# A carried state in 64 columns on four quarters of the array, and weight pieces that begin six rooms after their fetch

## The chip, the core and the metric

The kernel runs on one core of a Trainium2 chip. The core has a matrix engine (TensorE, PE in the profile; its weight loads are PEld), three engines for elementwise work (VectorE is DVE, ScalarE is ACT, GpSimd is POOL) and a queue processor (SyncE, SP) that issues most transfers between the memory of the chip and the on-chip buffer. TensorE writes its results to eight banks of an accumulator memory (PSUM), from which VectorE and ScalarE read them. Every engine works through its own list of instructions in order and waits at semaphores for the others. The metric is the device time of one execution in microseconds (us).

## What is computed

A retention layer with eight heads of 64 features, over two batches of 768 tokens, then two feed-forward layers on the 1536 x 512 result. Cut to what matters:

```python
# retention: per head, causal products with powers of lam, and a state carried from block to block
intra = einsum('bhij,bhjd->bhid', einsum('bhic,bhjc->bhij', qb, kb) * Dmask, vb)
inter = einsum('bhid,bhde->bhie', qb * lam_pow, kv_state)
out[:, :, sl] = intra + inter
kv_state = lam_block * kv_state + einsum('bhsd,bhse->bhde', kb * rev_pow, vb)
...
x = attn_out as [1536, 512]
h = maximum(x @ w_in, 0);  x = (h * h) @ w_out          # 512 -> 2048 -> 512
h = x @ w_in2;  out = maximum(0.01 * h, h) @ w_out2     # 512 -> 2048 -> 512
```

The four weight matrices are 64-bit floating-point numbers in memory.

## The kernel before

**Retention.** The work is cut into 12 units, six chunks of 128 tokens for each of two batches. The eight heads stand in four pairs (`NP` = 4): the two heads of a pair fill the 128 partitions, 64 features (`D`) each. All products here are in fp32, and the trace records each such matmul twice. Per unit there are `transposes` of k and q (line 294, copied to kT and qT by ScalarE on line 298), `scores` (line 311, one bank for each of the two heads of the pairs), `mask` (VectorE, line 316, makes Pm), `state` (line 335: the update of the carried state) and `output`. The state lies in two tiles `st` that alternate from chunk to chunk. They are 128 x 4 x 128: each pair has a 128 x 128 block of which only the two diagonal 64 x 64 blocks are filled and the rest stays zero (memset on line 321). So in `output` the product of the state with the scaled query qS (line 360) takes all 128 rows of the array and 64 of its columns, as the product of v with Pm does (line 362) that is added to it in the same bank; a pair of heads has two of each, one for either half of the columns. The bank is then cast to xhi by ScalarE (line 68) and the rest xlo is taken by VectorE (line 69), `split`. In the loop over the units, `state(i)`, `output(i)`, `mask(i + 1)` and `scores(i + 2)` follow each other on TensorE.

**The two MLPs.** All operands are split in a high and a low part, and each product takes three matmuls of 128 x 128 x 512 (`three`, line 503: high by high, high by low, low by high). Each layer goes through four stages of 512 hidden features; products of a stage go to `activate` (lines 468 to 486), which makes the operands g0h, g0l, g1h, g1l, sw of the second product. Some products are combined by sums and differences of tokens and weights (`four_sums`, lines 449 to 451, `weight_sums`, lines 437 to 442, and `activate_for_seven`, lines 482 to 491), so that fewer are needed.

**Weight pieces.** `fetch` starts the transfer of one 1 MB piece into one of two `raw` buffers. The generator `converting` then turns the 64-bit words to fp32: an absolute value on ScalarE (Abs, line 114), six steps on VectorE (lines 115 to 125), a cast to the high part on ScalarE (line 135) and a subtraction for the low part on VectorE (line 137). `convert` is called once for each room, a place in TensorE's program between half groups of matmuls: it takes the next step of a piece under way, or begins the next one that is fetched. Within the MLPs a piece's step fetches the next piece.

**What sets the order.** In the retention the order on SP and TensorE is the order in which the code is written, and in the MLPs that on TensorE. The order on VectorE, ScalarE and GpSimd is chosen by the framework's scheduler, unless an instruction is held in its place (`keep_in_program_order`), as the conversion steps are that the retention places.

## Time and profile before

| | |
|---|---|
| median of three runs | 576.34 us (575.51 to 576.9) |
| profiled execution | 577.1 us |
| its span, first to last instruction | 575.3 us |
| mean granted TensorE clock, share of full speed | 0.994 |
| TensorE matmul busy | 566.2 us |
| VectorE, ScalarE, GpSimd busy | 413.8, 303.7, 103.3 us |
| first matmul of the MLPs (line 503) starts at | 63.59 us |

All times in the trace are microseconds from the first instruction of the span. A time of the whole execution is 1.8 us more than the span. In a row of a timeline the columns are the start, the time, the engine, the line, the operation, what is written and read, the array shape on TensorE (128\*64 is 128 rows by 64 columns), sizes and the count; in brackets stands how long the engine was idle just before and what ended it. In a row of the chain they are the start, the time and what the time is put down to. The names are those of the program: `ps` a bank, `raw` a fetched piece, `hb` and `rb` a piece under conversion.

### The profile page before, as it was taken

What the parts mean: (1) busy time and instruction counts of PE and PEld (TensorE: products, weight loads), DVE (VectorE), ACT (ScalarE), POOL (GpSimd) and SP (SyncE); (2) the same over time, 40 slices, a digit from 0 to 9 for tenths busy, and PEclk for the clock granted to TensorE, in tenths of its full rate; (3) what the DMA queues carried; (4) which work ended last, traced back from release to release, by engine and by line L of the source; (5) the groups of instructions that cost most, each with busy time, mean ns of one, the idle gap of its engine ahead of it and who ended that gap; (6) DMA issues with size and microseconds to landing.
All of it is one profiled execution on the core that took longest, in us unless ns stands there. A gap on an engine that the chain in (4) does not pass through costs nothing.

```text
span 575.3 us, 8060 instructions
## 1 busy us (share of the span) xinstructions
PE 566.2 (98%) x3075; PEld 472.8 (82%) x3075; DVE 413.8 (72%) x579; ACT 303.7 (53%) x477; POOL 103.3 (18%) x115
## 2 busy tenths in 40 slices
PE   7999999999999999999999999999999999999997
PEld 6888888888788888888888888888888888888886
DVE  3588999999927599498478999929782996217222
ACT  2344598556757587757448375453562376225110
POOL 3659100000044503433000000000213010210000
PEclk9899999999999999999999999999999999999999
DMA  8998434665498957999513215341529423651432
GB/s 173 235 218 177 142 130 140 221 190 186 171 157 137 161 168 176 214 254 188 174 38 91 81 34 216 129 164 73 110 49 246 108 32 43 78 87 56 164 111 91
DMA packets 79350, 80.75 MB, mean 140 GB/s; under 512 B 40264, under 2 KB 51792, under 8 KB 79312
## 3 DMA queue, kind: packets, MB, share of 16 engines
q1 hardware_dynamic: 61312, 62.15, 35.2%
q0 software_dynamic: 17472, 17.83, 22.9%
q8 instruction: 24, 0.39, 0.3%
q10 hardware_dynamic: 528, 0.26, 0.2%
q14 instruction: 14, 0.11, 0.1%
HBM read 55.05 MB, written 30.42 MB: 149 GB/s over the span
## 4 chain that ended last, share of the span: by engine, by line
PE 79%; DVE 10%; DMA 5%; issue 3%; ACT 2%; POOL 1%; SPq 0%; ACTq 0%; POOLq 0%; DVEq 0%
PE ps L503 72%; DMA raw<-in_moe_w_in 4%; PE ps L294 2%; DMA raw<-in_moe_w_out 2%; DVE hb L118 2%; PE ps L311 1%; DVE rb L122 1%; DVE hb L125 1%; PE ps L362 1%; DVE hb L115 1%; DVE rb L121 1%; PE ps L335 1%; ACT hb L114 1%; PE ps L220 1%; PE ps L360 1%
## 5 line engine op out<-in xcount | busy, mean ns | idle before, releaser
L503 PE MATMUL ps<-xhi,w1h 128*128 128x512 f32 x288 | 112.2, 389 | 0.0
L503 PE MATMUL ps<-xhi,w1l 128*128 128x512 f32 x288 | 112.0, 389 | 0.0
L503 PE MATMUL ps<-xlo,w1h 128*128 128x512 f32 x288 | 112.0, 389 | 0.0
L616 POOL DMA_DIRECT2D spill<-f x48 | 47.1, 1194 | 348.3 <-ACT f L612 348.2
L612 ACT COPY f<-ps 128x512 f32<-128x512 f32 x84 | 48.4, 585 | 69.6 <-PE ps L503 68.8
L503 PEld LDWEIGHTS ps<-xhi,w1l 128*128 128x128 f32 x288 | 54.1, 188 | 11.3
L503 PEld LDWEIGHTS ps<-xlo,w1h 128*128 128x128 f32 x288 | 54.1, 188 | 11.3
L503 PEld LDWEIGHTS ps<-xhi,w1h 128*128 128x128 f32 x288 | 54.0, 188 | 11.3 <-issue 0.2
L474 DVE TENSOR_TENSOR g0l<-f,g0h 128x512 fp32r<-128x512 f32 x52 | 35.1, 687 | 32.5 <-ACT f L470 20.9
L503 PE MATMUL ps<-w2l,g0h 128*128 128x512 f32 (+1 forms) x132 | 50.5, 383 | 0.0
L503 PE MATMUL ps<-w2h,g0l 128*128 128x512 f32 (+1 forms) x132 | 50.5, 383 | 0.0
L503 PE MATMUL ps<-w2h,g0h 128*128 128x512 f32 (+1 forms) x132 | 50.5, 383 | 0.0
L114 ACT ACTIVATE hb<-raw 128x1024 f32<-128x1024 f32 x32 | 36.8, 1149 | 21.5 <-DVE w2l L137 8.3
L137 DVE TENSOR_TENSOR w2l<-hb,w2h 128x1024 fp32r<-128x1024 f32 x16 | 19.5, 1222 | 39.8 <-ACT w2h L135 39.8
L503 PE MATMUL ps<-g0h,w2h 128*128 128x512 f32 x104 | 40.5, 389 | 0.0
L503 PE MATMUL ps<-g0l,w2h 128*128 128x512 f32 x104 | 40.5, 389 | 0.0
L503 PE MATMUL ps<-g0h,w2l 128*128 128x512 f32 x104 | 40.5, 389 | 0.0
L122 DVE SCALAR_TENSOR_TENSOR rb<-raw,rb 128x1024 f32<-128x1024 uint32 x32 | 39.4, 1231 | 0.4
L125 DVE TENSOR_TENSOR hb<-hb,rb 128x1024 f32<-128x1024 f32 x32 | 39.4, 1231 | 0.4
L118 DVE SCALAR_TENSOR_TENSOR hb<-raw,hb 128x1024 uint32<-128x1024 uint32 x32 | 39.1, 1221 | 0.3
L567 DVE TENSOR_TENSOR f<-ps,f 128x512 f32<-128x512 f32 x40 | 26.2, 684 | 9.9 <-PE ps L503 9.9
L716 DVE TENSOR_TENSOR f<-ps,f 128x512 f32<-128x512 f32 (+1 forms) x25 | 16.7, 668 | 22.9 <-PE ps L503 22.8
(143 smaller groups left out, 1155.0 us busy)
## 6 DMA issues: line engine op xcount, KB each, us to landing
raw<-in_moe_w_in SPq DMA_DIRECT2D x16, 1024.0 KB, 5.7
raw<-in_moe_w_out SPq DMA_DIRECT2D x16, 1024.0 KB, 5.1
spill<-f POOLq DMA_DIRECT2D x48, 256.0 KB, 5.5
spill<-f SPq DMA_DIRECT2D x24, 256.0 KB, 2.8
f<-spill SPq DMA_DIRECT2D x24, 256.0 KB, 3.0
k<-in_k SPq DMA_DIRECT2D x12, 256.0 KB, 5.0
q<-in_q SPq DMA_DIRECT2D x12, 256.0 KB, 5.1
v<-in_v SPq DMA_DIRECT2D x12, 256.0 KB, 5.3
```

Of the source, the lines that this page charges most:

```text
L114: nc.scalar.activation(hf, w_hi.bitcast(F32), AF.Abs)
L118: yield ve.scalar_tensor_tensor(out=hb, in0=w_hi, scalar=0xC0000000, in1=hb, op0=ALU.bitwise_and, op1=ALU.bitwise_or)
L122: yield ve.scalar_tensor_tensor(out=rf, in0=w_lo, scalar=2.0 ** -52, in1=rf, op0=ALU.mult, op1=ALU.mult)
L125: yield ve.tensor_tensor(out=hf, in0=hf, in1=rf, op=ALU.add)
L137: yield ve.tensor_tensor(out=lo, in0=hf, in1=hi, op=ALU.subtract)
L294: nc.tensor.transpose(ps[:, p, :], src[:, 2 * p:2 * p + 2, :].rearrange("s h d -> s (h d)"), ident)
L474: nc.vector.tensor_tensor(out=glo, in0=r, in1=ghi, op=ALU.subtract)
L503: nc.tensor.matmul(ps, a, b, start=start and n == 0, stop=stop and n == len(ops) - 1, skip_group_check=again)
L567: ve.tensor_tensor(out=out, in0=ps[h, where], in1=other, op=ALU.add)
L612: nc.scalar.copy(f, src)
L616: nc.gpsimd.dma_start(dst, f, accum_op=ALU.add)
L716: nc.vector.tensor_tensor(out=a, in0=ps, in1=a, op=ALU.add)
```

## The change

The state tiles become 128 x 4 x 64: the blocks of the two heads of a pair lie in the upper and the lower 64 partitions, and there is no memset. The state is updated with one GpSimd and one VectorE operation on 128 partitions, where there were two each on 64.

In `output` the eight state products come first, then the eight value products. A state product now uses one quarter of the array, 64 rows by 64 columns: the rows are those of the head in its pair, the columns are the same half for even pairs and the other half for odd pairs. The output lies in two banks, even pairs in one and odd pairs in the other, and is split in two halves. For odd pairs the two halves of the 128 features are therefore swapped in xhi and xlo. To match, a piece of the first layer's w_in is fetched with three transfers: the even 128 rows in place, and for the odd ones each half of 64 rows to the other half of the partitions.

A fetched piece carries the count of rooms at which it may begin: six (`LAND`) after its fetch in the MLPs, and at once in the retention. The Abs is held in program order.

```diff
+    half = [slice(e * D, (e + 1) * D) for e in range(2)]
...
-            dma(r.rearrange("p (k f) -> p k f", k=k), source(*key))
-            fetched.append((key, r))
+            dst, src = r.rearrange("p (k f) -> p k f", k=k), source(*key)
+            if key[0] or key[2]:
+                dma(dst, src)
+            else:
+                dma(dst[:, 0:k:2], src[:, 0:k:2])
+                for a, b in ((half[0], half[1]), (half[1], half[0])):
+                    dma(dst[a, 1:k:2], src[b, 1:k:2])
+            fetched.append((key, r, len(rooms) + LAND if begun_mlp else 0))
...
-        nc.scalar.activation(hf, w_hi.bitcast(F32), AF.Abs)
+        tc.keep_in_program_order(nc.scalar.activation(hf, w_hi.bitcast(F32), AF.Abs))
...
     def convert(pin=False):
+        rooms.append(len(rooms))
...
-        if not fetched:
+        if not fetched or len(rooms) < fetched[0][2]:
             return
...
-            st.append(att.tile([P, NP, P], F32, name=f"st{e}"))
-            nc.gpsimd.memset(st[e], 0.0)
+            st.append(att.tile([P, NP, D], F32, name=f"st{e}"))
...
-                for par in range(2):
-                    r = slice(par * D, (par + 1) * D)
-                    nc.gpsimd.tensor_tensor(out=tmp[r], in0=old[r, :, r],
-                                            in1=LR[r, :, C - 1:C].to_broadcast([D, NP, D]), op=ALU.mult)
...
+                nc.gpsimd.tensor_tensor(out=tmp, in0=old, in1=LR[:, :, C - 1:C].to_broadcast([P, NP, D]), op=ALU.mult)
+                nc.vector.tensor_tensor(out=new, in0=ps, in1=tmp, op=ALU.add)
...
-            ps = bank().rearrange("p (a s) -> p a s", a=NP)
-            for p in range(NP):
-
-                rows = [slice(par * D, (par + 1) * D) for par in range(2)]
-                if c:
-                    for r in rows:
-                        nc.tensor.matmul(ps[r, p, :], st[c % 2][:, p, r], qS[n][:, p, :], start=True, stop=False)
-                for par, r in enumerate(rows):
-                    nc.tensor.matmul(ps[r, p, :], vn[:, 2 * p + par, :], Pm[n][:, par, p, :], start=c == 0, stop=True)
+            ps = [bank()[:, 0:2 * C].rearrange("p (a s) -> p a s", a=2) for _ in range(2)]
+            heads = [(p, par ^ p % 2) for p in range(NP) for par in range(2)]
+
+            def place(p, par):
+                return ps[p % 2][half[par ^ p % 2], p // 2, :]
+
+            if c:
+                for p, par in heads:
+                    nc.tensor.matmul(place(p, par), st[c % 2][half[par], p, :], qS[n][half[par], p, :],
+                                     start=p < 2, stop=False, skip_group_check=True)
+            for p, par in heads:
+                nc.tensor.matmul(place(p, par), vn[:, 2 * p + par, :], Pm[n][:, par, p, :],
+                                 start=c == 0, stop=True, skip_group_check=True)
...
-            split(xhi[t][:, :, o:o + C], xlo[t][:, :, o:o + C], ps)
+            for e in range(2):
+                split(xhi[t][:, e::2, o:o + C], xlo[t][:, e::2, o:o + C], ps[e])
```

Where this moves instructions is shown at three places, each as it stands before and then after. On TensorE, one unit of the retention: the scores, the transposes of a later unit, the state update and the output, of which before only the first of four pairs of heads stands here. (In these rows a name is what is written, then what is read, then the size of the result and how many in a row.)

```order
L311 MATMUL ps<-qT,kT 128x128 x8
L294 MATMUL ps<-ident,k 128x128 x4
L294 MATMUL ps<-ident,q 128x128 x4
L335 MATMUL ps<-v,kd 64x64 x8
L360 MATMUL ps<-qS,st_168 64x128 x2
L362 MATMUL ps<-Pm,v 64x128 x2
```

```order
L322 MATMUL ps<-qT,kT 128x128 x8
L305 MATMUL ps<-ident,k 128x128 x4
L305 MATMUL ps<-ident,q 128x128 x4
L345 MATMUL ps<-v,kd 64x64 x8
L366 MATMUL ps<-qS,st_168 64x128 x8
L369 MATMUL ps<-Pm,v 64x128 x8
```

The pairs of state and value products have become eight of one and then eight of the other. On ScalarE in the retention, where the first weight piece begins:

```order
L68 CAST xhi_278<-ps 128x4x128
L114 ACTIVATE hb<-raw 128x1024
L298 COPY kT<-ps 128x512
L298 COPY qT<-ps 128x512
L68 CAST xhi_278<-ps 128x4x128
```

```order
L68 CAST xhi_276<-ps 128x2x128 x2
L309 COPY kT<-ps 128x512
L309 COPY qT<-ps 128x512
L68 CAST xhi_276<-ps 128x2x128 x2
L124 ACTIVATE hb<-raw 128x1024
L309 COPY kT<-ps 128x512
L309 COPY qT<-ps 128x512
```

The Abs (L114, now L124) has moved behind the copies of kT and qT and the next unit's casts. On VectorE near the end of the second stage of the first MLP layer, the last of the sums by `activate_for_seven` (L491, now L500) and the subtraction that makes g1l (L69) from its cast:

```order
L488 TENSOR_TENSOR g0l<-f,g0h 128x512
L125 TENSOR_TENSOR hb<-hb,rb 128x1024
L491 TENSOR_TENSOR f<-f 128x512
L437 TENSOR_TENSOR rb<-hb 128x256
L438 TENSOR_TENSOR rb<-hb 128x256
L439 TENSOR_TENSOR rb<-rb,hb 128x256
L440 TENSOR_TENSOR rb<-hb,rb 128x256
L69 TENSOR_TENSOR g1l<-f,g1h 128x512
```

```order
L497 TENSOR_TENSOR g0l<-f,g0h 128x512
L131 TENSOR_SCALAR rb<-hb 128x1024
L500 TENSOR_TENSOR f<-f 128x512
L132 SCALAR_TENSOR_TENSOR rb<-raw,rb 128x1024
L69 TENSOR_TENSOR g1l<-f,g1h 128x512
L135 TENSOR_TENSOR hb<-hb,rb 128x1024
```

The four sums of a weight piece (L437 to L440) have left the place between them, and one conversion step (L132) stands there. The order of the matmuls in the MLPs is the same in both kernels.

## Rows read from the trace of the kernel before

**Rows 1.** The page: busy time, share of the span and instructions by engine

```profile
PE 566.2 (98%) x3075; PEld 472.8 (82%) x3075; DVE 413.8 (72%) x579; ACT 303.7 (53%) x477; POOL 103.3 (18%) x115
```

**Rows 2.** Waits of TensorE: us in total, times, longest

```profile
PE ps L335 <- POOL qS L304: 2.4, 1, 2.4
...
PE ps L503 <- DVE g1l L69: 0.9, 1, 0.9
```

**Rows 3.** The chain that ended last, from 64 us: its last piece

```profile
155.74 415.73 PE ps L503 x1844
```

**Rows 4.** Busy us of PE, PEld, DVE, ACT, POOL in two stretches of the MLPs

```profile
62.60:100.00 37.40, 37.40 (x179) 30.95 (x176) 36.91 (x48) 30.67 (x46) 0.00 (x0) 1.00 0.35 114
...
130.00:160.00 30.00, 29.08 (x128) 23.51 (x127) 29.45 (x42) 20.72 (x37) 1.03 (x1) 1.00 0.52 171
```

**Rows 5.** The chain from 14 to 64 us: units of the retention

```profile
33.86 1.03 PE ps L294 x8
34.88 0.61 PE ps L335 x16
35.50 0.22 PE ps L360 x4
35.72 0.22 PE ps L362 x4
...
37.25 1.09 PE ps L311 x16
...
39.36 0.37 PE ps L360 x4
...
43.99 0.88 PE ps L362 x16
```

**Rows 6.** TensorE's timeline, starts of outputs and of the scores behind them

```profile
26.12 0.39 PE L360 MATMUL ps<-qS,st 128*64 128x128 f32 x4
...
27.97 1.16 PE L311 MATMUL ps<-qT,kT 64*128 64x128 f32 x16
...
30.60 0.39 PE L360 MATMUL ps<-qS,st 128*64 128x128 f32 x4
...
32.69 1.16 PE L311 MATMUL ps<-qT,kT 64*128 64x128 f32 x16 [0.17 <-ACT qT L298]
```

**Rows 7.** ScalarE's timeline at the first weight piece

```profile
30.52 1.16 ACT L114 ACTIVATE hb<-raw 128x1024 f32<-128x1024 f32 x1 [1.85 <-DMA raw<-in_moe_w_in]
```

**Rows 8.** SP's timeline: issues of transfers

```profile
22.73 1.29 SPq L65 DMA_DIRECT2D raw<-in_moe_w_in  x1
...
26.00 4.25 SPq L65 DMA_DIRECT2D v<-in_v  x1
```

**Rows 9.** The tile v from 20 to 40 us: from issue to landing

```profile
DMA to landing us min/median/max: 4.8/5.8/7.3
```

**Rows 10.** TensorE's timeline from 153 to 157 us

```profile
153.95 0.88 PE L503 MATMUL ps<-g1h,sw 128*128 128x512 f32 x2
155.74 0.50 PE L503 MATMUL ps<-g1l,sw 128*128 128x512 f32 x1 [0.92 <-DVE g1l L69]
156.08 0.63 PE L503 MATMUL ps<-g1h,sw 128*128 128x512 f32 x2
```

**Rows 11.** VectorE's timeline in the same place

```profile
152.93 0.69 DVE L491 TENSOR_TENSOR f<-f 128x512 f32<-128x512 f32 x1
153.53 0.42 DVE L437 TENSOR_TENSOR rb<-hb 128x256 f32<-128x256 f32 x1
...
155.00 0.69 DVE L69 TENSOR_TENSOR g1l<-f,g1h 128x512 fp32r<-128x512 f32 x1
```

**Rows 12.** ScalarE's timeline in the same place

```profile
153.65 0.62 ACT L68 CAST g1h<-f 128x512 fp32r<-128x512 f32 x1 [1.82 <-DVE f L491]
```

**Rows 13.** VectorE from 64 to 170 us, groups: busy, mean ns

```profile
L122 DVE SCALAR_TENSOR_TENSOR rb<-raw,rb 128x1024 f32<-128x1024 uint32 x11 | 13.4, 1219 | 0.1
...
L115 DVE TENSOR_SCALAR hb<-hb 128x1024 f32<-128x1024 f32 x10 | 6.9, 687 | 0.4 <-ACT hb L114 0.4
```

**Rows 14.** ScalarE from 64 to 170 us, groups: busy, mean ns

```profile
L135 ACT CAST w2h<-hb 128x1024 fp32r<-128x1024 f32 x5 | 5.3, 1051 | 1.7 <-PE ps L503 0.9 <-DVE hb L125 0.7
```

More of the change, by code (lines that the diff above doesn't have):

```diff
@@ L86, in tile_retention_then_two_mlps @@
     todo = list(order)
-    fetched, at_work = [], []
+    fetched, at_work, rooms = [], [], []
+    LAND = 6
     wts, sums, opened = {}, {}, set()
@@ L94, in fetch @@
             k = 4 if key[2] == 0 else 2
-            dma(r.rearrange("p (k f) -> p k f", k=k), source(*key))
-            fetched.append((key, r))
+            dst, src = r.rearrange("p (k f) -> p k f", k=k), source(*key)
[6 more added lines that the diff above has]
+            fetched.append((key, r, len(rooms) + LAND if begun_mlp else 0))
     def converting():
-        key, r = fetched.pop(0)
+        key, r, _ = fetched.pop(0)
         l, s, n, h = key
@@ L339, in state @@
                 tmp = wk.tile([P, NP, D], F32, tag="tmp", name="tmp")
-                for par in range(2):
-                    r = slice(par * D, (par + 1) * D)
-                    nc.gpsimd.tensor_tensor(out=tmp[r], in0=old[r, :, r],
-                                            in1=LR[r, :, C - 1:C].to_broadcast([D, NP, D]), op=ALU.mult)
-            for par in range(2):
-                r = slice(par * D, (par + 1) * D)
-                if c:
-                    nc.vector.tensor_tensor(out=new[r, :, r], in0=ps[r], in1=tmp[r], op=ALU.add)
-                else:
-                    nc.vector.tensor_copy(new[r, :, r], ps[r])
+                nc.gpsimd.tensor_tensor(out=tmp, in0=old, in1=LR[:, :, C - 1:C].to_broadcast([P, NP, D]), op=ALU.mult)
+                nc.vector.tensor_tensor(out=new, in0=ps, in1=tmp, op=ALU.add)
+            else:
+                nc.vector.tensor_copy(new, ps)
         def output(n):
```

1 line of the change is left out of this document (removed).

## The prediction

> **What bounds the kernel now.** I read the busy shares of the page first: TensorE works 98% of the span [rows 1]. Then the table of its waits: two places stand out, 2.4 us in the first units, where the mask is not there yet, and 0.9 us in the long stage [rows 2]. The first lies ahead of all state products, and the change touches nothing that it waits for, so it stays. Third, the chain that ended last: from 155.74 on it is one piece of 1844 matmuls in 415.73 us, 0.2255 us each, with no hole [rows 3]. The number and order of these matmuls do not change. So a gain or loss can come from three places only: from the time TensorE spends per matmul in the retention (the chain from 14 to 64 us), from its few waits, and from waits that the new order of the other engines brings in. For the last, I looked at engine times by stage: VectorE is busy 36.91 of 37.40 us and 29.45 of 30 us in the two stretches of the first MLP stages that I show [rows 4], so it has no room there, though TensorE itself lacks only 0.92 us in the second.
>
> **Part 1, the state product.** In the chain each fp32 matmul is two records. One output of before takes four pairs of lines L360 and L362, each line 0.22 us for four records [rows 5], so its eight state products cost 4 x 0.22 = 0.88 us and its eight value products as much; alone they also take 0.88, at 43.99 [rows 5]. With an array half (128 rows by 64 columns) two of these run at once. On quarters four can, so eight take half: 0.44 us. The eight state updates of line L335, with half the columns, take 0.61 [rows 5], of which I put 0.15 down to the switch of shape before them (below); the rest, 0.46, shows that 16 records can be issued in that time. So the state products come to 0.44 to 0.46, a gain of 0.42 to 0.44.
>
> Against it stand switches of shape. A first L360 line after the transposes takes 0.37 where later ones take 0.22 [rows 5]: 0.15 for a change of shape. After L335, whose shape is the same as that of L360, the first line takes 0.22: no price. In after, the state products have a shape of their own, so an output that follows a state update pays twice (into quarters, and back to halves), one that follows transposes pays once more than now. Ten outputs have a state: two after transposes (units 1 and 5), seven after a state update, the last after the value products of the one before it. Eight gain 0.43 - 0.30 = 0.13, two gain 0.43 - 0.15 = 0.28: together **1.6 us**. What the trace does not show is a switch into quarters. Bounds: free, as from L335 to L360, all ten would gain 0.44, together 4.4; at 0.22, the dearest that I find (1.09 for the scores [rows 5], against 0.87 for eight matmuls two at a time), 2 x 0.22 = 0.4. I take 0.15, since transposes to halves is the nearest row.
>
> The state's smaller tile spares memsets, a GpSimd and a VectorE operation for each unit; an output is cast and split in two halves, one operation more on ScalarE and on VectorE. TensorE waits in the retention for none of these [rows 2], so I cost them at nothing; if that cover goes, a unit pays about one half operation.
>
> **Part 2, the absolute value held in place.** At 30.52 ScalarE starts the first piece's Abs, 1.16 us, after it has stood idle for a transfer [rows 7]; copies of the transposed k and q queue behind it, and the scores at 32.69 wait 0.17 for qT [rows 6]. From the start of an output to that of the next scores it is 1.85 us without a wait (26.12 to 27.97), and 2.09 here (30.60 to 32.69) [rows 6]: **0.24 us** lost. In after the Abs stands behind the next unit's casts. It finds its data there, and the copies that queue behind it then are wanted by scores 1.85 us of output later, so the wait goes: 0.24. For that piece SP issues three transfers where one was, with loads of k, q, v queued behind them. The one issue takes 1.29; the load of v that follows is itself held at 26.00 for 4.25 us, while the transfers ahead of it run [rows 8], and lands 7.3 us after its issue at the latest, at 33.3 [rows 9], while its first user runs at 34.88 [rows 5]. With TensorE some 0.8 us earlier there, 0.8 of that cover is left. Two more issues cost nothing while they vanish in the 4.25; wholly exposed (2 x 1.29) they would cost 2.6 - 0.8 = 1.8 us, my bound.
>
> **Part 3, pieces begun six rooms later.** The 0.9 of the waits table is more than 0.9. Around it, five matmuls (two, one and two) take from 153.95 to 156.08 + 2 x 0.227 = 156.53: 2.58 us instead of 5 x 0.227 = 1.13, a loss of **1.45 us** [rows 10]. The operand g1l that the middle one awaits is a subtraction on VectorE. Its input was cast on ScalarE from 153.65 to 154.27 [rows 12], but VectorE ran four sums of a weight piece from 153.53 to 155.00 first [rows 11], which is needed much later. In after's order those sums are elsewhere, and between the operation that feeds the cast and the subtraction stands one L132, the L122 of before, 1.22 us [rows 13], which covers the cast of 0.62. So this wait goes, 1.45 us. What is late next? The second half of the first w_out piece: its cast follows matmul 119 of the stage's count and its first use is matmul 150, where before 67 matmuls lay between. 31 matmuls are 7.0 us; an activation's three passes, a cast of 1.05 and a subtraction of 1.22 stand in them [rows 13, 14], and that fits. The longer way round, from matmul 83 (15.1 us), has Abs, both casts and six steps of VectorE, three of 1.22 and three of 0.69, with two activations between: by estimate 13.6, so 1.5 us spare. Every other piece has at least 49 matmuls.
>
> **Sum.** 1.6 + 0.24 + 1.45 = 3.3 us. The profiled execution took 577.1, 1.8 more than its span: 573.8 for one like it, span 572.0. The median of the runs is 0.76 lower: 576.34 - 3.3 = **573.0 us**. About 0.2% (1.15 us) is what a measurement of this kernel can tell from no change, so "faster" begins at 575.2.
>
> **Rivals.** *Only two quarters at a time.* Quarters of different rows, (0,0) and (64,64), write one bank in after, and the other two the other bank; the score products of before also use both row halves, but each half has its own bank, and no row shows two row halves on one bank. If such pairs take turns, the state products cost 0.88 as before and the switches come on top: 8 x 0.30 + 2 x 0.15 = 2.7 lost where 1.6 was won. 576.34 + 2.7 - 1.7 = 577.3 (578.6 with switches of 0.22). The Trainium skill, "TensorEngine Tiling (Array Packing)", section "Gotcha 1: PSUM Pressure", states that different row tiles cannot access the same bank at once; by that rule this rival would hold. The trace neither bears it out nor speaks against it. Chance 13%.
>
> *Slower: the quarters run one at a time.* Then eight cost 16 x 0.11 = 1.76 us, and each output loses 0.88 + switches: 8 x 1.18 + 2 x 1.03 = 11.5 lost. 576.34 + 11.5 - 1.7 = 586.1. It turns slower as soon as state products and switches together exceed 0.88 by 0.29 us for each output (2.85 over ten). Against it: halves do run side by side, in rows and in columns, in the trace. 5%.
>
> *Given back in the MLP.* VectorE has no room from 63 to 160 us [rows 4]. If its work, not its order, sets the pace, TensorE starts the MLP 1.8 us earlier only to wait there: 576.34 - 1.45 = 574.9, or, if the wait for g1l only moves to another operand, 576.3. For it: the 98% busy. Against it: VectorE had time for sums that nobody awaited before the one operand that was awaited, and its work begins earlier too when the products come earlier. 13%, half of it within 0.2% of before.
>
> *Switches free.* 4.4 in place of 1.6: 570.2, or some tenths more where the loads of v land late. Against it: each change of shape in the trace has a price. 7%.
>
> **How the numbers follow.** The forecast has 62%, with its own range from 571.9 to 574.6 (switches 0.10 to 0.22 each, some exposure of the issues). Faster: 62 + 7 + 6 of the third = 75%. Same: 7 of the third, 6 of the first rival, whose 577.3 is just within the bound = 13%. Slower: the rest, 12%. From 571.0 to 576.4 lie the forecast, the third rival and the upper end of the fourth: 80%.
>
> **What would show it.** In the chain of after, an output following a state update should read about 0.59 for eight state products and 1.03 for eight value products, and from the transposes to the scores of such a unit 0.13 less than the 3.39 of before (33.86 to 37.25); state products at 0.88 and more mean the first or second rival. No wait of the scores for qT before 33 us; no wait of L512 for g1l near 152 us; the first MLP matmul at 61.8 in place of 63.59. Any new row of waits on L512 (for w2h, w2l or g0l) is the third rival. I would be wrong if the wait for v grows with the three issues, or if TensorE gets a new wait in a later stage whose order I have not followed as closely as the first two.

## The result, and the profile after

The changed kernel is slower: 582.86 us (median of six runs, 579.46 to 584.57) against 576.67 for the kernel before in the same comparison, a ratio of 1.0104 with a 95% interval from 1.0075 to 1.0134. The forecast was 573.0 and a gain of 3.3 us; the median shows a loss of 6.2 us. The profiled execution of after took 584.57 us with a span of 582.8, and is the slowest of its six; its mean granted clock is 0.987, that of before 0.994. The page's line of busy times says nothing of the loss, TensorE is busy for 98% of the span as in [rows 1]:

```profile
PE 568.7 (98%) x3075; PEld 470.8 (81%) x3075; DVE 413.7 (71%) x581; ACT 304.7 (52%) x489; POOL 97.6 (17%) x105
```

The table of TensorE's waits does (us in total, times, longest). Before, the two places to look at were the wait for qS in the first units and the one for g1l [rows 2]. Now the g1l wait is gone, and five new ones have come, for g0l, g0h, k, q and v:

```profile
PE ps L512 <- DVE g0l L483: 3.5, 2, 2.3
PE ps L345 <- POOL qS L315: 2.3, 1, 2.3
...
PE ps L305 <- DMA k<-in_k: 1.4, 1, 1.4
PE ps L345 <- DMA v<-in_v: 0.7, 1, 0.7
PE ps L512 <- ACT g0h L478: 0.5, 1, 0.5
PE ps L305 <- DMA q<-in_q: 0.4, 1, 0.4
```

**The quarters do what was forecast.** In the chain of waits (start, time, what) an output that follows a state update (L345) now reads 0.60 for its eight state products (L366) and 1.02 for its eight value products (L369); forecast were 0.59 and 1.03. [rows 5] has the form of before.

```profile
49.44 1.02 PE ps L305 x8
50.46 0.62 PE ps L345 x16
51.08 0.60 PE ps L366 x16
51.67 1.02 PE ps L369 x16
52.70 1.09 PE ps L322 x16
```

**The retention loses at the loads.** SP's timeline shows the three transfers of the first weight piece, and the load of v held behind them, where [rows 8] has one transfer at 22.73:

```profile
22.85 2.77 SPq L65 DMA_DIRECT2D raw<-in_moe_w_in  x3
25.72 1.40 SPq L65 DMA_DIRECT2D k<-in_k  x1
27.21 0.53 SPq L65 DMA_DIRECT2D q<-in_q  x1
27.83 4.34 SPq L65 DMA_DIRECT2D v<-in_v  x1
```

The load of v was issued at 26.00 in before and landed 7.3 us later at the latest [rows 8, 9]; here it is issued at 27.83, and the chain counts 7.93 us until 35.76. TensorE, meanwhile, reaches the scores of this place at 31.02, where before it did at 32.69 [rows 6], and its timeline (start, time, line and operation; in brackets the idle time just before and what ended it) shows three waits in a row, for k, q and v:

```profile
31.02 1.16 PE L322 MATMUL ps<-qT,kT 64*128 64x128 f32 x16
33.54 0.63 PE L305 MATMUL ps<-ident,k 128*128 128x128 f32 x4 [1.36 <-DMA k<-in_k]
34.54 0.63 PE L305 MATMUL ps<-ident,q 128*128 128x128 f32 x4 [0.36 <-DMA q<-in_q]
35.90 1.12 PE L345 MATMUL ps<-v,kd 128*64 128x64 f32 x16 [0.74 <-DMA v<-in_v]
36.95 1.13 PE L366 MATMUL ps<-qS,st 64*64 64x128 f32 x16
38.01 1.98 PE L369 MATMUL ps<-Pm,v 128*64 128x128 f32 x16
```

These are 2.46 us of waits. The lines behind them then take about twice their time: 1.06 for L366 in the chain, 1.91 for L369, 2.01 for L322. The windows (busy us of PE, PEld, DVE, ACT, POOL, then the granted clock, the DMA share and GB/s) have the reason, a granted clock of 0.53, that is mostly the lower level of 1.2 GHz, from 35 to 40 us, behind those waits:

```profile
25.00:30.00 5.00, 5.00 (x93) 4.09 (x89) 2.88 (x6) 1.95 (x5) 3.19 (x4) 1.00 0.98 227
30.00:35.00 5.00, 3.27 (x44) 2.66 (x40) 1.81 (x4) 2.38 (x4) 2.54 (x3) 1.00 1.09 189
35.00:40.00 5.00, 4.26 (x52) 3.35 (x50) 2.35 (x5) 0.96 (x2) 1.04 (x1) 0.53 1.13 229
```

Against the same lines at full clock, the chain loses 0.51 + 0.46 + 0.89 + 0.92 + 0.10 = 2.88 us there. The first product of the MLPs starts at 66.28 instead of the forecast 61.8 (before: 63.59). Without the waits and the low clock it would have been 66.28 - 2.46 - 2.88 = 60.9.

**The MLPs lose at two activations.** TensorE's timeline has two places with holes, where [rows 10] had its one:

```profile
186.37 0.50 PE L512 MATMUL ps<-g0h,w2h 128*128 128x512 f32 x1 [0.46 <-ACT g0h L478]
189.19 0.80 PE L512 MATMUL ps<-g0l,w2h 128*128 128x512 f32 x1 [2.31 <-DVE g0l L483]
...
254.68 0.50 PE L512 MATMUL ps<-g0l,w2h 128*128 128x512 f32 x1 [1.14 <-DVE g0l L483]
```

The timelines of ScalarE and VectorE some microseconds earlier say why. ScalarE stands idle for 4.04 us at the held Abs (L124), until a weight piece has landed; an activation pass (L479) stands behind it. VectorE, which needs the Abs' result for its next step, is idle for 5.05 us:

```profile
178.00 1.12 ACT L124 ACTIVATE hb<-raw 128x1024 f32<-128x1024 f32 x1 [4.04 <-DMA raw<-in_moe_w_out]
179.03 0.62 ACT L479 ACTIVATE f<-f 128x512 f32<-128x512 f32 x1
```

```profile
179.15 0.69 DVE L125 TENSOR_SCALAR hb<-hb 128x1024 f32<-128x1024 f32 x1 [5.05 <-ACT hb L124]
...
188.45 0.68 DVE L483 TENSOR_TENSOR g0l<-f,g0h 128x512 fp32r<-128x512 f32 x1
```

From then on VectorE works without a break on what has piled up, and the g0l that TensorE awaits at 189 is only begun at 188.45. Behind that wait the granted clock is 0.89 from 185 to 190 us and 0.76 from 190 to 195. The second hole leads back in the same way, to an Abs at 247.85 that ScalarE awaits for 2.04 us. The chain puts the start of the first hole at the transfer, and after the second it reads as [rows 3] did, without one (324.61 / 1442 = 0.2251 us a matmul):

```profile
168.62 9.36 DMA raw<-in_moe_w_out
...
254.68 324.61 PE ps L512 x1442
```

The MLPs take 512.72 us from their first to their last product, where before took 507.59 with its one hole of 1.45.

### The profile page after: what moved, and what is told of

Its sections match the earlier page's. It is cut to its first block, busy times and chain, and to the rows that moved or that the text cites. A ratio compares the mean times of both kernels' runs of the same rounds, so it can differ in the third digit from the quotient of the medians.

```text
span 582.8 us, 8090 instructions
## 1 busy us (share of the span) xinstructions
PE 568.7 (98%) x3075; PEld 470.8 (81%) x3075; DVE 413.7 (71%) x581; ACT 304.7 (52%) x489; POOL 97.6 (17%) x105
## 4 chain that ended last, share of the span: by engine, by line
PE 75%; DMA 10%; DVE 6%; issue 5%; ACT 2%; POOL 1%; SPq 0%; DVEq 0%; ACTq 0%; POOLq 0%
PE ps L512 66%; DMA raw<-in_moe_w_out 3%; PE ps L369 2%; PE ps L322 2%; PE ps L305 2%; DMA partial10P<-f 1%; DMA v<-in_v 1%; DMA spill<-f 1%; DVE hb L128 1%; PE ps L345 1%; PE ps L366 1%; DMA spill<-partial10P 1%; DVE rb L132 1%; DMA partial10P<-partial10P 1%; DMA q<-in_q 1%
## 5 line engine op out<-in xcount | busy, mean ns | idle before, releaser
L512 PE MATMUL ps<-xhi,w1h 128*128 128x512 f32 x288 | 112.1, 389 | 0.0
L512 PE MATMUL ps<-xlo,w1h 128*128 128x512 f32 x288 | 112.0, 389 | 0.0
L512 PE MATMUL ps<-xhi,w1l 128*128 128x512 f32 x288 | 112.0, 389 | 0.0
L625 POOL DMA_DIRECT2D spill<-f x48 | 50.7, 1199 | 352.0 <-ACT f L621 351.5
L512 PEld LDWEIGHTS ps<-xhi,w1h 128*128 128x128 f32 x288 | 54.1, 188 | 11.4 <-PE ps L369 0.2
L512 PEld LDWEIGHTS ps<-xhi,w1l 128*128 128x128 f32 x288 | 54.1, 188 | 11.2
L512 PEld LDWEIGHTS ps<-xlo,w1h 128*128 128x128 f32 x288 | 54.1, 188 | 11.1
L512 PE MATMUL ps<-w2l,g0h 128*128 128x512 f32 (+1 forms) x132 | 50.5, 383 | 0.0
L512 PE MATMUL ps<-w2h,g0l 128*128 128x512 f32 (+1 forms) x132 | 50.5, 383 | 0.0
L512 PE MATMUL ps<-w2h,g0h 128*128 128x512 f32 (+1 forms) x132 | 50.5, 383 | 0.0
L512 PE MATMUL ps<-g0l,w2h 128*128 128x512 f32 x104 | 41.6, 400 | 3.5 <-DVE g0l L483 3.5
L483 DVE TENSOR_TENSOR g0l<-f,g0h 128x512 fp32r<-128x512 f32 x52 | 35.0, 686 | 10.8 <-ACT f L482 9.2
L512 PE MATMUL ps<-g0h,w2h 128*128 128x512 f32 x104 | 41.1, 395 | 0.5 <-ACT g0h L478 0.5
L512 PE MATMUL ps<-g0h,w2l 128*128 128x512 f32 x104 | 41.0, 394 | 0.0
L124 ACT ACTIVATE hb<-raw 128x1024 f32<-128x1024 f32 x32 | 36.4, 1138 | 8.6 <-DMA raw<-in_moe_w_out 6.1
L128 DVE SCALAR_TENSOR_TENSOR hb<-raw,hb 128x1024 uint32<-128x1024 uint32 x32 | 39.1, 1223 | 0.7
L132 DVE SCALAR_TENSOR_TENSOR rb<-raw,rb 128x1024 f32<-128x1024 uint32 x32 | 39.1, 1222 | 0.6
L125 DVE TENSOR_SCALAR hb<-hb 128x1024 f32<-128x1024 f32 x32 | 22.6, 706 | 17.8 <-ACT hb L124 17.7
```

What stands on the lines that cost most here:

```text
L124: tc.keep_in_program_order(nc.scalar.activation(hf, w_hi.bitcast(F32), AF.Abs))
L125: yield ve.tensor_scalar(out=hf, in0=hf, scalar1=2.0 ** -15, scalar2=122368.0, op0=ALU.max, op1=ALU.min)
L128: yield ve.scalar_tensor_tensor(out=hb, in0=w_hi, scalar=0xC0000000, in1=hb, op0=ALU.bitwise_and, op1=ALU.bitwise_or)
L132: yield ve.scalar_tensor_tensor(out=rf, in0=w_lo, scalar=2.0 ** -52, in1=rf, op0=ALU.mult, op1=ALU.mult)
L483: nc.vector.tensor_tensor(out=glo, in0=r, in1=ghi, op=ALU.subtract)
L512: nc.tensor.matmul(ps, a, b, start=start and n == 0, stop=stop and n == len(ops) - 1, skip_group_check=again)
```

## The experiments

The table has every kernel that ran: median, ratio to before with its interval (before was 576.2 to 577.0 in all batches), and from the one profiled execution the start of the MLPs and their length. Profiles of one program differ: e6 and after have the same list of instructions on every engine, and their profiled executions start the MLPs at 62.34 and 66.28, with and without the spell of low clock. A start is therefore read together with its waits, and one profile can stand apart from the median of its kernel: that of after is the slowest of its six runs, that of e6 the fastest of its five, that of e9 the fastest of its ten. e3, e9 and e17 leave the swap out of the first layer; they stand for times only.

| kernel | median us | ratio | MLPs start | MLPs last |
|---|---|---|---|---|
| before | 576.67 | 1 | 63.59 | 507.59 |
| after | 582.86 | 1.0104 [1.0075, 1.0134] | 66.28 | 512.72 |
| e1 quarters and three transfers, no rooms, no hold | 580.33 | 1.0068 [1.0036, 1.01] | 62.58 | 511.21 |
| e2 before, with rooms and hold | 582.64 | 1.0088 [1.0061, 1.0115] | 62.85 | 514.23 |
| e3 after, one transfer | 580.99 | 1.0063 [1.0035, 1.009] | 61.35 | 514.40 |
| e4 after, first fetch a unit later | 584.25 | 1.0121 [1.008, 1.0163] | 64.93 | 513.36 |
| e5 after, no hold | 581.38 | 1.0071 [1.0042, 1.0101] | 63.46 | 510.77 |
| e6 after, no rooms | 581.79 | 1.0092 [1.0062, 1.0122] | 62.34 | 510.07 |
| e7 one transfer, swap in the transposes | 591.51 | 1.0248 [1.0207, 1.0289] | 76.40 | 512.08 |
| e8 before, three transfers | 580.97 | 1.0072 [1.0043, 1.01] | 64.25 | 510.63 |
| e9 quarters only, one transfer | 578.51 | 1.004 [1.0025, 1.0054] | 61.45 | 508.18 |
| e10 two transfers, hold in the retention only | 577.03 | 1.001 [0.9992, 1.0029] | 64.85 | 506.94 |
| e11 the two a unit apart or more | 579.1 | 1.0043 [1.0027, 1.0059] | 67.51 | 507.07 |
| e12 the same, a unit later | 577.26 | 1.0009 [0.9993, 1.0024] | 65.65 | 506.58 |
| e13 first piece in four transfers | 591.92 | 1.0263 [1.0242, 1.0283] | 78.89 | 507.92 |
| e14 the four in four units | 590.73 | 1.0252 [1.0231, 1.0274] | 77.02 | 507.24 |
| e15 two pieces in four | 610.49 | 1.0593 [1.0575, 1.0611] | 98.5 | 506.73 |
| e16 the four, a unit later | 591.46 | 1.0258 [1.024, 1.0276] | 77.54 | 508.32 |
| e17 e9, first piece in two full transfers | 580.42 | 1.0066 [1.0043, 1.0089] | 62.12 | 511.82 |
| e18 e10, issued from ScalarE's queue | 579.37 | 1.0044 [1.0029, 1.0059] | 66.11 | 507.96 |

### What each part does alone: e1, e2, e3, e4

e1 is after without the rooms and the hold:

```diff
-    LAND = 6
+    LAND = 0
-        tc.keep_in_program_order(nc.scalar.activation(hf, w_hi.bitcast(F32), AF.Abs))
+        nc.scalar.activation(hf, w_hi.bitcast(F32), AF.Abs)
```

> The change without its second part: quarters, split output and three transfers stay, LAND is 0 and the Abs is not held. Theory: the loss has two sources, late loads in the retention (first MLP matmul at 66.3 instead of 61.8 us) and, in the MLPs, an Abs held in front of the activations while its piece has not landed (TensorE waits near 186 and 253 us). Then this kernel keeps the first alone: MLP start 65 to 66.5, no wait for g0l of over 1 us, median 579 to 580.5. Rival: the waits in the MLPs come from the three transfers that delay w_out behind them: then they stay, 582 to 583.5.

The MLPs start 1.0 us earlier than in before, with 1.5 us of waits for k, q and v left in. But they last 3.6 us longer, by holes at 153 (g1h and g1l) and 218.

e2 is before with those two lines of after alone (`LAND = 6` and the held Abs):

> The kernel before with LAND = 6 and the Abs held, nothing else. Theory (an Abs held before its piece has landed stops the activations): MLP start 63.3 (no wait for qT), the g1l wait gone, but waits for g0l of 1 to 4 us in all with a low clock behind them: median 577 to 581. Rival (the three transfers cause these waits): none here, 576.7 - 0.24 - 1.45 = 575.0.

The result is as slow as after, with nothing changed in the retention's products or transfers. The row of its ScalarE is the one of after again, an Abs that the engine stands waiting at, and the wait for g0l behind it is TensorE's largest:

```profile
174.85 1.12 ACT L115 ACTIVATE hb<-raw 128x1024 f32<-128x1024 f32 x1 [4.33 <-DMA raw<-in_moe_w_out]
```

```profile
PE ps L505 <- DVE g0l L476: 3.7, 3, 2.4
```

e3 is after with one transfer for each piece, which leaves the swapped halves out of the first layer:

```diff
-            if key[0] or key[2]:
-                dma(dst, src)
-            else:
-                dma(dst[:, 0:k:2], src[:, 0:k:2])
-                for a, b in ((half[0], half[1]), (half[1], half[0])):
-                    dma(dst[a, 1:k:2], src[b, 1:k:2])
+            dma(dst, src)
```

> The change with every w_in piece of the first layer fetched in one transfer, without the swap of halves (this part of the product is left wrong). Theory A, three issues push the loads of k, q and v back: MLP start 61.8, no wait for k or v, and with the waits of the MLPs as they are 578 to 579. Theory B, a faster TensorE overtakes loads that are limited by bytes, which this kernel moves too: waits for k and v stay at half or more of their 2.5 us, MLP start 64 to 66, 581 to 583.

The MLPs start at 61.35, within half a microsecond of the forecast 61.8. That is partly chance: the wait in the first units is 1.3 us here, where the forecast left 2.4 standing, and v is awaited for 1.0. But the waits for k and q are gone with the two extra transfers. The loss in the MLPs is that of e2.

e4 fetches the first piece one unit later and makes up for the missed conversion steps later on:

```diff
-            if i in (1, 9):
+            if i in (2, 9):
```

> The change with its first weight piece fetched one unit later, behind the loads of k, q and v that came late (its conversion begins two units later and takes two steps a unit). Both theories of the loads: no wait for k6, q6 and v4, so no low clock there; MLP start 61.5 to 63, median 578 to 580, if the piece's 1 MB does not make the next loads late instead (then MLP start stays above 64).

It did not help: k, q and v are awaited as before (0.9, 0.9, 0.7 us), and a wait of 1.4 for xlo has joined them.

### Hold, rooms and transfers apart: e5, e6, e8

e5 takes only the hold out of after (the second pair of lines of e1's diff), e6 only the rooms (the first pair).

> The change with LAND = 6, but the Abs free for the scheduler to place. Theory H, the held Abs stops the activations behind it while its piece is under way: no wait for g0l of over 1 us, the MLPs within 507 to 510 us, median 577.5 to 580 (the late loads of the retention stay). Theory L, six rooms leave too little time for the rest of a conversion, wherever the Abs stands: waits of 3 us and more stay near 186 and 253 us, MLPs 511 to 514, median 581 to 583.

> The change with the Abs held and LAND = 0, so that a held Abs stands earlier, nearer to the issue of its transfer. Theory H: longer and more waits behind a held Abs than with six rooms, MLPs 514 to 525, median 583 to 595. Theory L: no more of these waits, MLPs 507 to 511, median 577.5 to 580.5.

Neither theory had it right. Row by row, the instruction lists of e6 are those of after, and the lists of e5 those of e1. The six rooms change nothing at all in either pair: gone through in the kernel's code room by room, none of the 32 pieces has reached its turn before six rooms have passed. So e2 too is in effect the hold alone. What moves VectorE's and ScalarE's work is the hold, and, as e8 shows, the transfers.

e8 is before with three transfers for a w_in piece (the same sizes, nothing swapped):

```diff
-            dma(r.rearrange("p (k f) -> p k f", k=k), source(*key))
+            if key[0] or key[2]:
+                dma(dst, src)
+            else:
+                dma(dst[:, 0:k:2], src[:, 0:k:2])
+                for a in (slice(0, D), slice(D, P)):
+                    dma(dst[a, 1:k:2], src[a, 1:k:2])
```

> The kernel before with each w_in piece of the first layer in three transfers, without a swap. If the two further issues push the loads back by the 2.5 us seen in the change (v of unit 4 lands at 35.8), TensorE at its old pace waits 0.5 to 1.5 us for k, q and v between 33 and 36 us: MLP start 64.1 to 65.5, median 577 to 578.5. If the loads only come late for a faster TensorE: MLP start 63.6, median 576.4.

The transfers alone cost 4.0 us (ratio 1.0072): in the profile 0.66 in the retention, and 3.0 in the MLPs. There the scheduler has put another order on VectorE. Its timeline at the place of [rows 11] now has two conversion steps (L127, L128) between the last sum (L497) and the subtraction that makes g1l, and TensorE waits. But VectorE also comes to that sum a microsecond later than in before (153.97 against 152.93), having waited 4.0 us for an Abs since 60 us, against 1.4 in before. How much of the 3.0 is the order and how much the lateness, these rows do not part:

```profile
153.97 0.68 DVE L497 TENSOR_TENSOR f<-f 128x512 f32<-128x512 f32 x1
154.57 0.68 DVE L127 TENSOR_SCALAR rb<-hb 128x1024 uint32<-128x1024 uint32 x1
155.29 1.23 DVE L128 SCALAR_TENSOR_TENSOR rb<-raw,rb 128x1024 f32<-128x1024 uint32 x1
156.43 0.69 DVE L69 TENSOR_TENSOR g1l<-f,g1h 128x512 fp32r<-128x512 f32 x1
```

```profile
157.17 0.50 PE L509 MATMUL ps<-g1l,sw 128*128 128x512 f32 x1 [1.31 <-DVE g1l L69]
```

### Keeping the gain: e7, e9, e10, e11, e12

e9 is the quarters alone: one transfer, no rooms, no hold (again without the swap).

> Quarters with one transfer for each w_in piece (features of odd pairs left unswapped, so this part of the product is wrong), no rooms, the Abs not held. VectorE's order around the awaited g1l is that of the kernel before (four sums ahead of it). Theory: the loss of the change lies in the three transfers and in the order that they and the held Abs bring, not in the quarters: MLP start 61.3, MLPs 507.6 as before, median 574.2 to 575. Rival, given back in the MLPs: VectorE, with no room to 160 us, does not follow an earlier start: MLPs 509.5 and more, median 576 to 579.

Its profiled run, the fastest of ten, took 575.19 and looks as the theory said: the MLPs start at 61.45 and last 508.18, with one hole at 152 in them. But the median is 2.3 us above before, in the range of the rival; the other nine runs took 577.58 to 580.72 and have no trace. e17 (below) shows what can happen with the same order of work: its lists for VectorE, ScalarE and GpSimd are those of e9. A w_out piece landed 7.8 us after its issue there, in e9 5.9; VectorE stood idle longer for that piece's Abs, reached the last sum before g1h at 154.12 instead of 151.40, and TensorE waited longer for g1h. First e9, then e17:

```profile
114.70 0.69 DVE L119 TENSOR_SCALAR hb<-hb 128x1024 f32<-128x1024 f32 x1 [0.35 <-ACT hb L118]
152.79 0.50 PE L505 MATMUL ps<-g1h,sw 128*128 128x512 f32 x1 [0.61 <-ACT g1h L68]
```

```profile
117.36 0.69 DVE L123 TENSOR_SCALAR hb<-hb 128x1024 f32<-128x1024 f32 x1 [2.25 <-ACT hb L122]
155.50 0.50 PE L509 MATMUL ps<-g1h,sw 128*128 128x512 f32 x1 [2.54 <-ACT g1h L68]
```

That is the condition of the prediction's third rival: a VectorE with no room hands a late transfer on. That it is what makes the nine other runs of e9 longer is not shown.

e7 makes the swap on TensorE instead, with transposes that are written as products with the identity, 64 columns at a time, so that a whole piece can come in one transfer:

```diff
-                    nc.tensor.transpose(ps[:, p, :], src[:, 2 * p:2 * p + 2, :].rearrange("s h d -> s (h d)"), ident)
+                    for e in range(2):
+                        nc.tensor.matmul(ps[half[e], p, :], src[:, 2 * p + (e ^ p % 2), :], ident, start=True, stop=True)
```

> Quarters without swapped features and without the three transfers: the heads of odd pairs stand swapped in kT, qT and the state instead, by transposes of 64 columns each (fp32 products with the identity, on halves of the array). LAND 0, Abs not held. The transposes then have the shape of the state update, so one switch a unit less: 10 x 0.15 = 1.5 us. MLP start 61.35 (one transfer, e3) - 1.5 = 59.8 if the loads allow it, 61.4 if loads set the pace. In the MLPs waits for g1h and g1l as in e1 (0 to 5 us): median 573.5 to 578.

It is the wrong trade: the MLPs start 12.8 us later than in before. In its chain the two sets of transposes of a unit read 1.90 us in place of 1.02, where the clock is full. Not all of the 12.8 is theirs: at 33.41 TensorE waits 5.31 us for qT, whose copy stands behind an Abs that ScalarE awaits for 5.93 us, and the granted clock is 0.57 and 0.74 in the two windows from 30 to 40 us. The row of the transposes:

```profile
41.59 1.90 PE ps L305 x32
```

e10 gives the heads 0 to 3 the lower and 4 to 7 the upper 64 columns, so that the swap is undone by two transfers, each of the 512 rows' halves to 64 partitions, and holds the Abs in the retention alone:

```diff
+                rows = source(*key, raw=True)
+                for e in range(2):
+                    dma(dst[half[e]], rows[e * 4 * D:(e + 1) * 4 * D].rearrange("(k p) f -> p k f", p=D))
...
-            heads = [(p, par ^ p % 2) for p in range(NP) for par in range(2)]
+            heads = [(p, par) for a in range(2) for par in range(2) for p in (a, a + 2)]
...
-                return ps[p % 2][half[par ^ p % 2], p // 2, :]
+                return ps[par][half[p // 2], p % 2, :]
```

> The change with heads 0 to 3 in the lower and 4 to 7 in the upper half of the output's partitions, so that a w_in piece takes two transfers of 64 partitions, not three; the two banks then belong to the two row halves; no rooms; the Abs held in the retention only. In the order of VectorE one conversion step stands ahead of g1l. Theory: MLPs 506.3 to 508, MLP start 61.4 to 63.5 (one issue more than e3), median 573 to 576.5. Rival (any other order than that of before brings new waits): MLPs 510 to 512, median 577 to 581.

This one is no slower than before (1.001 [0.9992, 1.0029]). Its MLPs last 506.94, 0.65 less than those of before, with one small hole left; but the retention gives it back. The MLPs start at 64.85, later than the forecast 61.4 to 63.5: k and v are awaited longer than in after:

```profile
PE ps L307 <- DMA k<-in_k: 2.5, 2, 1.9
PE ps L347 <- DMA v<-in_v: 1.4, 2, 0.9
```

e11 issues the two transfers in units 1 and 3, e12 in units 2 and 4, with the conversion steps moved accordingly.

> As e10, with the two halves of the first piece fetched two units apart (after the loads of the second and of the fourth turn of the loop), its conversion begun one unit later. If loads of k, q and v pushed back by 1 MB are what TensorE waits for: MLP start 61.0 to 62, 0.5 to 1.5 us better than e10, median 572.5 to 575. If the bytes count whenever they come: as e10.

> As e11, each half one turn later, behind more of the loads. If the loads have gained room by then: MLP start as e11 or up to 0.5 better; if not, waits for k, q and v of 1 us and more between 36 and 46 us, and the median 1 to 3 us over e11's.

Spreading them did not make the loads punctual, and neither expectation was met. In e12 the waits for k, q and v add up to 4.4 us, spread over more units. e12 is on a par with before, e11 slower.

### What delays the loads: e13 to e18

Two theories were left: more issues on SP's queue, or transfers that fill only 64 partitions. e13 fetches the first piece of e10's layout in four transfers over all 128 partitions, whose source has two blocks of 64 rows.

```diff
+                    for kk in range(4) if part is None else part:
+                        dma(dst[:, kk], rows.rearrange("(e k p) f -> k e p f", e=2, k=4)[kk])
```

> As e10, the first piece in four transfers over all 128 partitions (one for each chunk of features) at the same place, where e10 has two over 64. Theory I, the number of issues pushes the loads of k, q and v back: four issues instead of two, MLP start 64.8 or later, waits for k, q, v of 5 us and more. Theory R, transfers over half the partitions move fewer bytes in a time: MLP start 61.4 to 63, waits under 2 us.

That did not tell the two apart, it brought something worse: k is awaited for 15.5 us, and while the four transfers run the DMA engines are busy for a fifth of this window and move 59 GB/s in it:

```profile
25.00:30.00 5.00, 5.00 (x99) 4.23 (x96) 2.68 (x7) 2.16 (x5) 2.99 (x4) 1.00 0.20 59
```

The Trainium skill, "DMA: Bandwidth & Descriptors", section "Why a DMA increments its semaphore by 16 and not by 1", states that a transfer is spread over as many engines, up to 16, as divide the outermost size of both its patterns; with an outermost size of two that would be two engines. The trace agrees in kind, with a share of 0.20 where the other kernels have about 1 in that window. e14 (the four in units 1 to 4), e16 (in units 2 to 5) and e15 (two pieces so) share the pattern and its price, and miss their forecasts by it. In e15 TensorE waits 19.4 us at one place, for a carried state that VectorE makes behind the second piece's Abs.

> As e13, one of the four transfers behind each of the first four units' loads, the conversion from the fifth on, two steps a unit at the end. If 1 MB in one go is what the loads cannot bear: waits for k, q, v under 1 us, MLP start 60.8 to 62, MLPs 507 to 508.6, median 573.5 to 575.5, faster than both kernels. If bytes or issues count wherever they stand: MLP start as e10 (64 to 65), median 576 to 578.

> As e14, the second piece in four transfers too, which changes the order of VectorE: no conversion step that delays g1l (MLPs 506.3 to 507.2), but the last state update of the retention stands behind a conversion step (TensorE waits some 1.3 us near 61). Median within 1 us of e14.

> As e14, each transfer one turn of the loop later. If the loads gain room over TensorE with each unit: waits for k, q, v smaller than in e14, MLP start up to 1 us earlier; if their room is largest at the start, the other way round.

e17 is e9 with the first piece in two transfers that each fill all 128 partitions:

```diff
+            if key == (0, 0, 0, 0):
+                dma(dst[:, 0:2], src[:, 0:2])
+                dma(dst[:, 2:4], src[:, 2:4])
+            else:
+                dma(dst, src)
```

> The kernel of e9_one_free (quarters, one transfer over 128 partitions per piece, nothing held in place, the swap of the sixteen-row blocks left out), with the first w_in piece alone fetched in two transfers of 128 partitions (two of the four row groups each). One more issue, no 64-partition transfer. If the number of issues delays the loads of k, q and v behind the piece, the first MLP product comes at 63 to 65 us (e9: 61.45, e10 with two 64-partition transfers: 64.85) and the waits on k, q, v add up to 2 us or more. If the 64-partition transfers are to blame, it stays at 61.2 to 62.2 us, with waits as in e9. The MLPs as in e9 or up to 2 us longer; median 577.5 to 580 by the second, 580 to 582 by the first.

e18 is e10 with the two half transfers issued from ScalarE's queue, so that SP has no extra issue:

```diff
+                    if not begun_mlp and key[3] == 0:
+                        tc.keep_in_program_order(nc.scalar.dma_start(d_, s_))
```

> The kernel of e10_two_transfers (heads 0 to 3 on the lower, 4 to 7 on the upper half of the array; two 64-partition transfers per piece), with the two transfers of the pieces fetched during retention issued from ScalarE's queue, held at their place in its program, where e10 issues them on SyncE's between the loads of k, q and v. If what delays those loads is that SyncE has two issues more to make ahead of them, the first MLP product comes at 61.5 to 63 us (e10: 64.85), the waits on k and v of e10 (2.5 and 1.4 us) go below 1 us together, and the median is 573.5 to 575.5. If the half-partition transfers keep the rings busy longer, the loads are as late from either queue: 64 to 66 us and 576.5 to 578.

Against the number of issues speaks e17: with one issue more it has no wait for k, q or v, and its MLPs start at 62.12 with a wait of 1.3 for qT in them. e17 and e10 both issue two transfers and then the load of k at nearly the same time; in e17 that load lands 6.9 us after its issue, in e10 8.9. First e17, then e10, each with the line for k's landing:

```profile
22.55 1.71 SPq L65 DMA_DIRECT2D raw<-in_moe_w_in  x2
24.36 0.41 SPq L65 DMA_DIRECT2D k<-in_k  x1
DMA to landing us min/median/max: 6.9/6.9/6.9
```

```profile
22.26 1.92 SPq L65 DMA_DIRECT2D raw<-in_moe_w_in  x2
24.29 0.55 SPq L65 DMA_DIRECT2D k<-in_k  x1
DMA to landing us min/median/max: 8.9/8.9/8.9
```

e18, with no extra issue on SP, still waits 2.3 us for q and 0.4 for v, and starts at 66.11. It is the weaker witness, since its two transfers go out at 20.48 and 21.23 us, some 2 us earlier than those of e10. And what e17 shows of an extra issue is shown for the loads only: its median is 580.42, and its MLPs last 3.6 us longer than those of e9, where up to 2 was expected. The windows from 25 to 30 us, in which the piece comes in, show the rate as their last number; loads of k, q and v are in it too. First e17, then e18:

```profile
25.00:30.00 5.00, 5.00 (x94) 4.09 (x90) 2.47 (x5) 0.87 (x3) 2.85 (x3) 1.00 1.15 310
```

```profile
25.00:30.00 5.00, 3.02 (x48) 2.31 (x40) 2.96 (x7) 1.23 (x3) 2.72 (x3) 1.00 1.16 200
```

The same window has 312 GB/s in before and 292 in e9, all with pieces over 128 partitions; 227 in after, 251 in e6 and 244 in e8, where half of the piece comes in transfers over 64, and 218 in e10, where all of it does, as in e18. The DMA engines are as busy in both groups (0.98 to 1.16): the half transfers keep them occupied and move less. The Trainium skill, "SBUF — State Buffer", section "Door 1: The DMA port swizzle", states this rule: 64 neighbouring partitions reach only half of the on-chip buffer's ports, and it gives 196 GB/s for them against 328 for 128 partitions. The trace agrees with the rates above; which port is the limit no run here shows.

## Why the prediction was wrong

**Part 1, the state products: right.** 0.60 and 1.02 against 0.59 and 1.03, and from transposes to scores of a unit with both 3.26 us (49.44 to 52.70), 0.13 less than in before, as forecast. The first two rivals fall: quarters of different rows write one bank at once, so the rule of "Gotcha 1: PSUM Pressure" in the Trainium skill's "TensorEngine Tiling (Array Packing)" is not borne out for these products. e10 tests it directly: there each bank has quarters of the same rows, and the chain reads 0.60 for eight state products as well. "Switches free" falls too. Over the whole retention, from the scores at 19.48 in before and 18.45 in e9 to the first product of the MLPs, and less the waits between, it is 43.9 against 42.2 us: 1.7 won, where 1.6 was forecast. Of the three pairs with and without quarters, all else alike, one shows a gain in the medians: e3 is 1.65 us below e2, but e1 and e5 are level with e8, and e9 is 2.3 above before.

**Part 2, the held Abs: the sign was wrong.** The step "so the wait goes: 0.24" looked at the first piece only. There it held, in part: behind the piece e9, without the hold, waits 0.77 us for qT, and e3, with it, not at all; but e3 waits 0.23 and 0.79 for v instead, and both start the MLPs at the same time. I never asked what the hold does to the other pieces. In the MLPs a held Abs makes ScalarE wait for its piece (4.33 us in e2, 4.04 in after) with activation passes behind it, and the hold alone costs 514.23 - 507.59 = 6.6 us in the MLPs of before, and 6.2 in its median (e2). With quarters and one transfer it is 6.2 in the MLPs of the two profiles (e3 against e9), but 2.5 between the medians, since e9's is not as fast as its profile. With three transfers it makes no more difference than the runs scatter: e5 without it 581.38, e6 with it 581.79. There the free Abs has holes of its own.

**Part 2, the loads: the term was mis-sized.** The text priced the extra issues, at nothing or at 1.8 us at most, "while they vanish in the 4.25". One issue more did not delay them (e17). The term that was missing is the transfers' rate: 312 GB/s in the window became 227, and TensorE, faster by the right Part 1, came 1.7 us earlier to loads that were 2.5 us later (35.76 against 33.3). Waits of 2.46 us and 2.88 us of low clock behind them are the whole distance of 4.5 us between 61.8 and 66.28, and 0.9 more. These 0.9 TensorE had won in the first units (the third unit's transposes start at 15.83 instead of 16.74), by luck as it seems: the granted clock from 14 to 16 us was 0.72, in the profile of before 0.50, and in e6, which is the same program as after, 1.00. That the wait for v might grow with the three transfers stood among what would make the prediction wrong.

**Part 3, the rooms: cause wrong, row right.** The wait for g1l near 152 is gone, as the order said: one conversion step (L132) stands ahead of the subtraction. But the rooms had no part in it: they hold no piece back (e6). It went with the hold, which put new and longer waits at 186 and 254. The text gave the reading only for the first two stages and named just this as a risk; "any new row of waits on L512 is the third rival" is what came, at more than its price: that rival had the gain given back, 574.9 to 576.3, and not a loss. So the chance of 12% for slower was too small. The mechanism that made it slower, an engine held at a transfer that has not landed, was not among the rivals. The condition of the third rival itself, a VectorE without room, can be seen in e17 beside e9.

**The sum for the profiled execution.** Forecast 573.8, measured 584.57. The later start gives 66.28 - 61.8 = 4.5, the longer MLPs 512.72 - 506.14 = 6.6 (506.14 is 507.59 less the 1.45 that should have gone), and 0.3 less lies behind the last product: 10.8. That is the slowest execution of after; the fastest of e6, the same program, has 62.34 and 510.07, and a typical one should lie between. In the range, switches at 0.10 give 576.34 - 2.6 - 1.69 = 572.05, not 571.9, which changes nothing here.

What stays open: what makes nine of e9's runs slower than its profile; why the scheduler orders VectorE anew when only transfers change; and whether a layout with full transfers and the MLP order of e10 would gain. The start of e3, the MLPs of e10 and the 3.8 and 1.8 us behind their last product would give 61.35 + 506.94 + 5.6, about 574, by estimate, but no run had both.

## What to carry to other kernels

When a change splits a transfer, price the transfers by the partitions that each of them fills and not by the number of issues, and look at who becomes early where they become late. An instruction that is held in place must be followed at every place where it stands: an engine that works in order and waits at a transfer also holds what queues behind it. An engine with no time to spare, as VectorE here, passes on most of what it waits (e17). A wait of TensorE can cost twice its length, since a spell of low clock may follow it (2.46 and 2.88 us here).

## What the runs showed of the hardware

- Four quarters of the array ran at once on two banks, two quarters of different rows on each: eight fp32 state products in 0.60 us, of which 0.15, by estimate, goes to the change of shape. With quarters of the same rows on each bank (e10) it is 0.60 as well.
- In the windows in which the first weight piece came in, 200 to 251 GB/s were moved where all or half of it was in transfers over 64 partitions, and 292 to 312 where all of it was over 128, with the DMA engines equally busy.
- While transfers over 128 partitions with a source of two blocks ran, a window had 59 GB/s and a DMA share of 0.20 (e13).
- An instruction held at its place until its transfer had landed kept ScalarE idle for 4.33 us (e2) and 4.04 us (after), and the engines behind it late.
- Eight fp32 transposes of 128 columns take 1.02 us; written as sixteen products with the identity on 64 columns they take 1.90.
- Behind 2.46 us of waits for k, q and v TensorE had a granted clock of 0.53 from 35 to 40 us in after; behind 2.40 us of them at the same place, in e5, it kept 1.00.
